# Attention plus gated MLP on one core: the second batch's q loaded ahead of the weights, w_sg in two loads, paired loads for the last batch, and a new written order of steps

## Chip, core and metric

The kernel runs on one core of one Trainium2 chip. The metric is the device time in microseconds of one execution. Engines are named as in the profile: PE is TensorE's matmuls and PEld its weight loads, DVE is VectorE, ACT is ScalarE, POOL is GpSimd and SP is SyncE, which here only issues DMAs. TensorE writes its results into PSUM, and other engines have to copy them out before the PSUM buffer can be used again.

## What is computed

There are two layers, one behind the other, on 4 batches of 768 positions. First comes attention with 8 heads of 64, where each position sees the last 128 positions and the first 4 ("sinks"):

```
scores = (q @ k^T) / 8;  keep = (pos_k < 4) | (0 <= pos_q - pos_k < 128)
a = softmax(where(keep, scores, -1e9));  x[b, s, 64*h:64*h+64] = a @ v
```

Then comes a gated MLP on x (768 x 512 for each batch):

```
h = gelu_tanh(x @ w_in)                     # 512 -> 1024, halves u and v of 512
v_n = (v - mean(v)) / sqrt(var(v) + 1e-6) * g_ln
v_s = w_sg @ v_n + b_sg                     # mixes the 768 positions
out = x + (u * v_s) @ w_out                 # 512 -> 512
```

All inputs are float32 in device memory. The matmuls run in bf16, and the loads that POOL issues convert on the way.

## The kernel before, in words

The whole program is one long list of short steps, the string STEPS (lines 16 to 64). Each step is a small function, called once with the numbers behind its name: batch first, then head pair, tile or half. The order of the list is the order of issue on every engine: each engine works through its own share of the list strictly in order, and what ties the engines together are semaphore waits that follow from who reads and writes which buffer. There is no scheduler at run time. A trailing letter A, D or P says which engine (ACT, DVE, POOL) does a copy, a mask or a product.

**Attention.** Heads go in pairs, four pairs p = 0..3 for each batch. LQ and LK load q and k (lines 191 to 213), LV loads v (line 216). For batches 0 to 2 (letter S in TURN, line 72), TQ and TK turn q and k with 12 TensorE transposes a pair (line 304), and EQ and EK copy the result out of PSUM (lines 221 and 223). For batch 3 (letter D) SP turns them with a DMA transpose (line 314), from buffers qn and kn; those are loaded one head at a time (line 198), two loads for each pair. KS picks the four sink columns of k (line 329), SK multiplies them with q (lines 338 and 344), SX takes the exponential (349). QK makes scores for two key tiles of one pair (358), EX takes the exponential (366), MK masks (DVE 373, POOL 377 and 381), AV multiplies with v for one half of the positions (398, 404, 408), and NR divides by the row sum and writes x (417, 418).

**MLP.** XT and XE turn x on TensorE and copy it out (427, 221/223); for batches 2 and 3 XD does it with a DMA transpose on SP (435). MV and MU are the two halves of x @ w_in (444, 496), with MA and UA as first parts of them, GV and GU their gelu (458, 512). BN, RS, NM and Z normalise v (467 to 487); RS is on POOL (475). WT and WE turn w_sg, six row tiles, once (519, 524). SP multiplies with w_sg (529), GT adds the bias (534), GM multiplies with u (539), OU multiplies with w_out (545), RA adds x (553), ST stores (556). HM(n) puts n extra matmuls of nothing ahead of a step (183).

**What sets the order.** PSUM is used through two rings of buffers: "sc" with 2 (QK, MV, MU) and "mm" with 4 (all other matmul results). The step that takes a buffer of a ring waits until the copy or product that read its last contents is done. The masked scores P have a ring of 8. The 1152 KB of w_sg arrive in one load (LWS, line 239) in a buffer that GM's products use later.

**POOL as a DMA queue.** Almost all loads are issued by POOL, in line with its masks, products and RS. There are eight DMA semaphores for them, handed out in turn, so a load waits until the load eight before it has landed, and everything behind it on POOL waits too:

```
   def LWS():
        return nc.gpsimd.dma_start(out=wsg_rows, in_=moe_w_sg.rearrange("(c p) f -> p c f", p=128))
```

The order of the loads before is: q and k of batch 0, v of batch 0, w_in (two halves, LW), w_sg, w_out (LWO), then q and k of batch 1 for pairs 0-1, v of batch 1, q and k of batch 1 for pairs 2-3, and so on. q and k of batches 1 and 2 come in loads of four heads (384 KB in bf16), v in loads of two heads (192 KB).

Of the kernel before, what the change touches and what calls it, by code (L numbers as in the profile page):

```python
# [9 lines left out]
BF16 = mybir.dt.bfloat16  # L10
# [18 lines left out]
GM.0.1.0.D LV.2.1 SP.0.0.1 GT.0.1.1 EK.1.1.A MK.1.0.0 QK.1.0.1 QK.1.0.2 GT.0.0.1 GM.0.1.1.P TQ.1.2 EX.1.0.1 TQ.1.3
EQ.1.2.D TK.1.3 GM.0.0.1.P EX.1.0.2 QK.1.1.1 TK.1.2 EK.1.3.D EQ.1.3.A MK.1.0.1.P QK.1.1.2 SP.0.1.3 EK.1.2.A MK.1.0.2.D  # L30
LQ.2.2 EX.1.1.1 SP.0.0.2 KS.1.0 LK.2.2 EX.1.1.2 GT.0.1.3 SK.1.0 LV.2.2 GT.0.0.2 QK.1.2.2 SX.1.0 QK.1.1.0 MK.1.1.2.D
SP.0.1.2 LV.2.3 EX.1.1.0 MK.1.1.1.D AV.1.0.1 EX.1.2.2 GM.0.1.3.P GT.0.1.2 AV.1.1.1 NR.1.0.1 GM.0.0.2.P QK.1.3.0 TK.2.0
NR.1.1.1 EX.1.3.0 TK.2.1 LQ.3.0 MK.1.2.2.D QK.1.3.2 TQ.2.1 EK.2.1.A EK.2.0.D QK.1.3.1 EQ.2.1.A SP.0.0.3 MK.1.3.0
LK.3.0 GM.0.1.2.D AV.1.0.0 GT.0.0.3 TQ.2.0 EX.1.3.1 NR.1.0.0 OU.0.5 MK.1.1.0 EX.1.3.2 LV.3.0 TQ.2.2 RA.0.5 EQ.2.0.A
TQ.2.3 QK.1.2.1 MK.1.3.2.D ST.0.5 QK.1.2.0 EQ.2.3.A AV.1.1.0 EQ.2.2.D MK.1.3.1.P OU.0.3 EX.1.2.0 NR.1.1.0 AV.1.3.0
EX.1.2.1 TK.2.3 RA.0.3 TK.2.2 LQ.3.1 NR.1.3.0 EK.2.3.A ST.0.3 QK.2.0.1 QK.2.0.0 MK.1.2.0 AV.1.3.1 EK.2.2.A XT.1.2
MK.1.2.1.P EX.2.0.1 NR.1.3.1 OU.0.4 XE.1.2.D EX.2.0.0 MK.2.0.1.P AV.1.2.0 RA.0.4 AV.1.2.1 NR.1.2.0 QK.2.0.2 ST.0.4
QK.2.1.1 EX.2.0.2 XT.1.0 LK.3.1 EQ.3.0 KS.2.0 XT.1.1 EX.2.1.1 SP.0.0.0 XE.1.0.D NR.1.2.1 MK.2.0.2.P QK.2.1.2 QK.2.1.0
XE.1.1.D SK.2.0 EX.2.1.2 MK.2.1.1.P GT.0.0.0 XT.1.3 EK.3.0 SX.2.0 MV.1.0 GM.0.0.0.D LV.3.1 XE.1.3.A MK.2.0.0 EX.2.1.0
MK.2.1.2.D LQ.3.2 AV.2.0.0 GM.0.0.3.D GV.1.0 MK.2.1.0 MV.1.2 EQ.3.1 LK.3.2 OU.0.2 LV.3.2 GV.1.2 BN.1.0 MV.1.1 LQ.3.3  # L40
EK.3.1 RA.0.2 OU.0.0 BN.1.2 GV.1.1 MU.1.2 ST.0.2 RA.0.0 RS.1.2 EQ.3.2 OU.0.1 GU.1.2 BN.1.1 LK.3.3 MU.1.1 LV.3.3 NM.1.2
MU.1.3 RA.0.1 GU.1.1 ST.0.0 EK.3.2 RS.1.1 Z.1.4.A NR.2.0.0 MU.1.0 Z.1.5.A NM.1.1 GU.1.3 Z.1.1.D AV.2.0.1 Z.1.2.D
GU.1.0 AV.2.1.1 Z.1.3.D ST.0.1 QK.2.2.0 Z.1.0.A NR.2.0.1 QK.2.2.1 AV.2.1.0 EX.2.2.0 NR.2.1.1 SP.1.1.0 NR.2.1.0
SP.1.0.3 GT.1.1.0 GM.1.1.0.D EQ.3.3 EX.2.2.1 SP.1.0.2 MK.2.2.0 GT.1.0.3 QK.2.3.1 MK.2.2.1.P QK.2.3.0 GT.1.0.2 EX.2.3.1
SP.1.0.1 EK.3.3 GM.1.0.3.D GM.1.0.2.D EX.2.3.0 AV.2.2.0 MK.2.3.1.P GT.1.0.1 SP.1.1.2 NR.2.2.0 QK.2.2.2 GM.1.0.1.D
QK.2.3.2 SP.1.0.0 MK.2.3.0 EX.2.2.2 GT.1.1.2 EX.2.3.2 AV.2.3.0 MK.2.2.2.D QK.3.1.0 GT.1.0.0 MK.2.3.2.P QK.3.0.2
AV.2.2.1 EX.3.1.0 NR.2.3.0 SP.1.1.1 GM.1.0.0.P EX.3.0.2 NR.2.2.1 XD.2.0 AV.2.3.1 GM.1.1.2.D MK.3.0.2.P GT.1.1.1 OU.1.2
NR.2.3.1 GM.1.1.1.P QK.3.1.1 RA.1.2 QK.3.1.2 OU.1.1 EX.3.1.1 MK.3.1.0 EX.3.1.2 SP.1.1.3 KS.3.0 ST.1.2 XD.2.1 RA.1.1
MK.3.1.2.P SK.3.0 QK.3.0.0 GT.1.1.3 SX.3.0 QK.3.0.1 OU.1.0 MK.3.1.1.D EX.3.0.0 GM.1.1.3.P AV.3.1.0 EX.3.0.1 RA.1.0
MV.2.0 MK.3.0.0 ST.1.0 MK.3.0.1.D ST.1.1 OU.1.3 GV.2.0 OU.1.5 RA.1.3 MV.2.2 ST.1.3 BN.2.0 MV.2.1 GV.2.2 RA.1.5 BN.2.2  # L50
ST.1.5 MU.2.2 GV.2.1 OU.1.4 BN.2.1 GU.2.2 RS.2.2 MU.2.0 NM.2.2 RS.2.1 RA.1.4 MU.2.3 GU.2.0 NR.3.1.0 ST.1.4 MU.2.1
Z.2.5.D GU.2.3 NM.2.1 Z.2.4.D Z.2.1.A Z.2.2.D AV.3.0.1 Z.2.0.D GU.2.1 QK.3.2.0 NR.3.0.1 AV.3.1.1 EX.3.2.0 Z.2.3.D
# [22 lines left out]
def kernel(  # L79
# [14 lines left out]
    nc = tc.nc  # L94
# [188 lines left out]
    def ZERO():  # L283
        for t in v_sb:
            nc.vector.memset(t[:, :, :, Dh:Dh + 1], 1.0)
        for t in ks_sink:
            nc.vector.memset(t, 0.0)
# [337 lines left out]
```

## Time and profile before

| | |
|---|---|
| median of 4 runs | 160.19 us (159.74 to 160.43) |
| the profiled execution | 159.3 us, of which the span of the profile is 157.6 us |
| TensorE clock granted, mean | 0.995 |
| busy in the span | PE 146.8, DVE 128.6, ACT 100.7, POOL 87.0 us |
| loads issued by POOL | 45600 packets, 77.3% of 16 engines' span |
| transfers issued by SP | 17648 packets, 28.0% |

Times in the profile count from the span's start. Busy time of PE is a union of pipelined matmuls, each of which is shown longer than the distance to the next one: six matmuls of SP are 0.97 us apart from start to start of the next group, though one is shown as 326 ns. Where the text below adds up matmul work, it uses these distances. A landing time of a load is the start of its issue plus the time from issue to landing.

### The profile page before, as it was taken

What the parts mean: (1) busy time and instruction counts of PE and PEld (TensorE: products, weight loads), DVE (VectorE), ACT (ScalarE), POOL (GpSimd) and SP (SyncE); (2) the same over time, 40 slices, a digit from 0 to 9 for tenths busy, and PEclk for the clock granted to TensorE, in tenths of its full rate; (3) what the DMA queues carried; (4) which work ended last, traced back from release to release, by engine and by line L of the source; (5) the groups of instructions that cost most, each with busy time, mean ns of one, the idle gap of its engine ahead of it and who ended that gap; (6) DMA issues with size and microseconds to landing.
All of it is one profiled execution on the core that took longest, in us unless ns stands there. A gap on an engine that the chain in (4) does not pass through costs nothing.

```text
span 157.6 us, 3835 instructions
## 1 busy us (share of the span) xinstructions
PE 146.8 (93%) x1522; PEld 86.7 (55%) x1522; DVE 128.6 (82%) x305; ACT 100.7 (64%) x118; POOL 87.0 (55%) x118
## 2 busy tenths in 40 slices
PE   4878989989999999999999999999999999999970
PEld 1444566655566667554575655455656644556530
DVE  4479899998699999959979997779899936976861
ACT  3689995369997798795599658655975124670000
POOL 7998890244899995998923485004046400409120
PEclk9999999999999999999999999999999999999998
DMA  5999999999999999999999159431001581030154
GB/s 160 171 186 165 195 209 209 206 233 178 180 198 173 196 153 213 187 173 140 210 218 174 17 100 152 169 116 66 5 0 24 115 265 69 0 120 14 55 184 166
DMA packets 63266, 22.70 MB, mean 144 GB/s; under 512 B 51472, under 2 KB 60176, under 8 KB 63248
## 3 DMA queue, kind: packets, MB, share of 16 engines
q0 software_dynamic: 45600, 11.80, 77.3%
q1 hardware_dynamic: 17648, 10.66, 28.0%
q8 instruction: 12, 0.20, 0.5%
q14 instruction: 6, 0.05, 0.1%
HBM read 24.81 MB, written 6.29 MB: 197 GB/s over the span
## 4 chain that ended last, share of the span: by engine, by line
PE 61%; DMA 24%; POOL 9%; issue 1%; DVE 1%; POOLq 1%; DVEq 0%
PE mm L529 16%; DMA k<-in_k_dram 13%; PE mm L545 12%; PE sc L496 11%; DMA v_sb<-in_v_dram 11%; PE sc L444 10%; PE sc L358 4%; PE mm L398 3%; POOL v_sb L216 2%; POOL k L194 2%; POOL q L194 2%; PE mm L404 2%; PE mm L408 1%; PE mm L304 1%; PE mm L427 1%
## 5 line engine op out<-in xcount | busy, mean ns | idle before, releaser
L366 ACT ACTIVATE P<-sc 128x1024 bf16<-128x1024 f32 (+1 forms) x48 | 43.6, 962 | 10.1 <-PE sc L358 9.3
L529 PE MATMUL mm<-wsgT,z 128*128 128x384 bf16 x192 | 34.2, 326 | 0.0
L529 PEld LDWEIGHTS <-z 128*128 128x128 bf16 x192 | 17.8, 98 | 12.2 <-issue 1.3
L545 PE MATMUL mm<-w_out_sb,wsg_gated 128*128 128x512 bf16 (+1 forms) x100 | 23.7, 371 | 0.9 <-POOL wsg_gated L539 0.9
L534 DVE SCALAR_TENSOR_TENSOR gtmp<-mm,g_sb,b_bc 128x384 bf16<-128x384 f32 x32 | 19.4, 613 | 4.6 <-PE mm L529 4.6
L496 PE MATMUL sc<-xT,w_in_sb 128*128 128x384 bf16 x128 | 22.8, 326 | 0.0
L444 PE MATMUL sc<-w_in_sb,xT 128*128 128x512 bf16 x96 | 22.5, 379 | 0.1
L553 DVE TENSOR_TENSOR ot<-mm,x_sb 128x512 f32<-128x512 f32 (+1 forms) x25 | 16.5, 666 | 7.3 <-PE mm L545 7.2
L373 DVE TENSOR_TENSOR P<-P,mask 128x1024 bf16<-128x1024 bf16 (+1 forms) x31 | 22.0, 725 | 0.4 <-ACT P L366 0.3
L377 POOL TENSOR_SCALAR_AFFINE_SELECT P<-P 128x512 bf16<-128x512 bf16 x17 | 11.1, 656 | 19.0 <-ACT P L366 12.7
L539 POOL TENSOR_TENSOR wsg_gated<-gtmp,uT 128x384 bf16<-128x384 bf16 x16 | 15.4, 966 | 11.1 <-DVE gtmp L534 11.0
L216 POOL DMA_DIRECT2D v_sb<-in_v_dram x16 | 16.5, 1040 | 7.1 <-DMA wsg_gated<-in_moe_w_sg_dram 5.5
L458 ACT ACTIVATE vt<-sc 128x1024 f32<-128x1024 f32 x12 | 12.2, 1023 | 12.5 <-PE sc L444 12.5
L512 ACT ACTIVATE uT<-sc 128x768 bf16<-128x768 f32 x16 | 12.7, 805 | 10.4 <-PE sc L496 10.4
L475 POOL TENSOR_TENSOR rs<-rs,neg_half 128x4 f32<-128x4 f32 (+1 forms) x8 | 7.1, 886 | 21.5 <-DVE rs L470 19.6
L418 DVE TENSOR_TENSOR x_sb<-mm,rcp 128x384 bf16<-128x384 f32 x32 | 17.8, 558 | 1.1
L467 DVE BATCH_NORM_STATS2 st<-vt 128x6 f32<-128x512 f32 x24 | 16.2, 674 | 2.9 <-ACT vt L458 2.9
L358 PE MATMUL sc<-qT,kT 64*128 64x256 bf16 x192 | 15.3, 263 | 2.2 <-ACT P L366 1.4
L496 PEld LDWEIGHTS <-w_in_sb 128*128 128x128 bf16 x128 | 12.3, 98 | 9.0
L398 PEld LDWEIGHTS <-P 128*128 128x128 bf16 x192 | 14.7, 98 | 4.5 <-issue 2.2
L398 PE MATMUL mm<-v_sb,P 128*128 128x65 bf16 x192 | 16.5, 194 | 0.3
L404 PE MATMUL mm<-v_sb,P 128*128 128x65 bf16 x160 | 15.5, 194 | 0.0
(73 smaller groups left out, 222.3 us busy)
## 6 DMA issues: line engine op xcount, KB each, us to landing
out_dram<-ot SPq DMA_DIRECT2D x23, 256.0 KB, 2.4
v_sb<-in_v_dram POOLq DMA_DIRECT2D x16, 192.0 KB, 9.5
q<-in_q_dram POOLq DMA_DIRECT2D x4, 384.0 KB, 15.9
k<-in_k_dram POOLq DMA_DIRECT2D x4, 384.0 KB, 14.7
wsg_gated<-in_moe_w_sg_dram POOLq DMA_DIRECT2D x1, 1152.0 KB, 15.9
w_in_sb<-in_moe_w_in_dram POOLq DMA_DIRECT2D x2, 512.0 KB, 9.9
qn<-in_q_dram POOLq DMA_DIRECT2D x8, 96.0 KB, 6.0
kn<-in_k_dram POOLq DMA_DIRECT2D x8, 96.0 KB, 5.5
```

The lines of the kernel that those rows point to most:

```text
L216: return nc.gpsimd.dma_start(out=v_sb[b % len(v_sb)][:, 2 * p:2 * p + 2, :, 0:Dh].rearrange("p h t d -> p (h t) d"), in_=v[b, 2 * p:2 * p ...
L358: nc.tensor.matmul(sc[:, hl, 256 * jl:256 * jl + n], kT[b, p][rows, 128 * j:128 * (j + 1)], qT[b, p][rows, 128 * j:128 * j + n], start=Tru ...
L366: nc.scalar.activation(out=pt[:, :, 0:w], in_=sc_ring[b, p, g][:, :, 0:w], func=AF.Exp, scale=scale)
L373: nc.vector.tensor_mul(pt[:, :, 0:w], pt[:, :, 0:w], m.unsqueeze(1).to_broadcast([128, 2, w]))
L398: nc.tensor.matmul(av[:, il, hl, :], P[b, p, i // 2][:, hl, 256 * (i % 2):256 * (i % 2) + 128], vb[:, h, i, :], start=first, stop=False)
L404: nc.tensor.matmul(av[:, il, hl, :], P[b, p, j // 2][:, hl, 256 * (j % 2) + 128:256 * (j % 2) + 256], vb[:, h, j, :], start=False, stop=False)
L418: nc.vector.tensor_mul(xs[:, 3 * half:3 * half + 3, 128 * p:128 * (p + 1)].rearrange("p t (h d) -> p t h d", h=2), av[:, :, :, 0:Dh], rcp. ...
L444: nc.tensor.matmul(hp[:, jl, :], xT[b][:, j, c, :], w_in_sb[:, c, d_half:2 * d_half], start=(c == 0), stop=(c == KD - 1))
L496: nc.tensor.matmul(hp[:, n, 0:NH], w_in_sb[:, c, 128 * dc:128 * (dc + 1)], xT[b][:, 3 * hf:3 * hf + 3, c, :], start=(c == 0), stop=(c == K ...
L529: nc.tensor.matmul(ps[:, 0:NH], z[b][:, si, 128 * dc:128 * (dc + 1)], wsgT[:, si, NH * hf:NH * (hf + 1)], start=(si == 0), stop=(si == NT ...
L534: nc.vector.scalar_tensor_tensor(out=gtmp.new((b, hf, dc)), in0=mm_ring["g", b, hf, dc][:, 0:NH], scalar=g_sb[:, dc:dc + 1], in1=b_bc[:, N ...
L545: nc.tensor.matmul(mm_ring["o", b, t][:, cols], gatedT[:, (2 * b + hf) % 3, dc, 128 * tl:128 * (tl + 1)], w_out_sb[:, dc, cols], start=(dc ...
```

## The change

The steps' functions stay as they are except for these:

- LWS takes a number: w_sg comes in two loads of three row tiles (576 KB each).
- For batch 3, q and k of two pairs now share one buffer (qn and kn have 2 buffers of twice the size), and a load brings two heads for it instead of one: 8 loads of 192 KB instead of 16 of 96 KB. A pair of batch 3 then holds heads 0 and 2, or 1 and 3 of the four, and AV and NR address its two heads with a stride (heads()).
- The sink product of batch 3 follows from that: KS writes into a new buffer ks_far, which ZERO clears with one more memset, and SK makes two accumulating matmuls of 64 columns for each half of the 128 rows, where it made four of 32 columns.
- LG, the load of b_sg, waits for the first half of w_sg, where it waited for the whole.
- The branch for letter R, which no batch used, is gone.

The list of steps is written anew. In its loads: POOL masks come ahead of the third load, q of batch 1, pairs 0-1, is loaded ahead of the last v load of batch 0 and of w_in; q and k for the other pairs of batch 1 follow right behind w_sg; w_out comes behind k of batch 1, v of batch 1 behind the first q of batch 2, and v of batch 2 ahead of its k. The first two casts of q and k (CQ, CK) go from ACT to DVE. Work given to engines, before and after, in steps:

| | before | after |
|---|---|---|
| copies of turned q and k (EQ, EK) on ACT / DVE | 15 / 9 | 17 / 7 |
| casts CQ, CK on ACT / DVE | 2 / 0 | 0 / 2 |
| masks (MK) on DVE / POOL | 31 / 17 | 28 / 20 |
| products (GM) on DVE / POOL | 16 / 16 | 15 / 17 |
| normalising (Z) on ACT / DVE | 10 / 14 | 9 / 15 |
| extra matmuls (HM) | 10 | 8 |

The core of the diff:

```diff
-HOLDS = "LG<LWS"
+HOLDS = "LG<LWS.0"
...
-    qn = Ring("qn", 4, [128, NT, 2, Dh], BF16)
-    kn = Ring("kn", 4, [128, NT, 2, Dh], BF16)
+    qn = Ring("qn", 2, [128, 2, NT, 2, Dh], BF16)
+    kn = Ring("kn", 2, [128, 2, NT, 2, Dh], BF16)
...
     def rows(ring, src, b, p):
-        t = ring.new((b, p))
-        return [nc.gpsimd.dma_start(out=t[:, :, hl, :], in_=src[b, 2 * p + hl].rearrange("(t p) d -> p t d", p=128))
+        t = ring.new((b, p // 2))
+        return [nc.gpsimd.dma_start(out=t[:, :, :, hl, :].rearrange("p k t d -> p (k t) d"),
+                                    in_=src[b, 2 * p + 2 * hl:2 * p + 2 * hl + 2].rearrange("h (t p) d -> p (h t) d", p=128))
                 for hl in range(2)][-1]
+
+    def heads(b, p):
+        return slice(2 * p - p % 2, 2 * p - p % 2 + 3, 2) if TURN[b][p] == "D" else slice(2 * p, 2 * p + 2)
...
-    def LWS():
-        return nc.gpsimd.dma_start(out=wsg_rows, in_=moe_w_sg.rearrange("(c p) f -> p c f", p=128))
+    def LWS(i):
+        return nc.gpsimd.dma_start(out=wsg_rows[:, NG * i:NG * (i + 1), :],
+                                   in_=moe_w_sg[128 * NG * i:128 * NG * (i + 1), :].rearrange("(c p) f -> p c f", p=128))
...
-        for t in ks_sink:
+        for t in (*ks_sink, ks_far):
             nc.vector.memset(t, 0.0)
...
         ps = fresh(mm_ring, ("s", b, p0))
         for p in range(HP):
+            if TURN[b][p] == "D":
+                r0 = 64 * (p // 2)
+                nc.tensor.matmul(ps[r0:r0 + 64, :], ks_far[:, 64 * p:64 * p + 64], qT[b, p][:, 256:768],
+                                 start=(p % 2 == 0), stop=(p % 2 == 1))
+                continue
```

The first part of the list, up to the first SP step, before:

```
 ZERO IDEN LQ.0.0 LK.0.0 LQ.0.1 FILL LK.0.1 LC MASK LQ.0.2 MASK0 CQ.0.0.A VSK LK.0.2 HM.7 TQ.0.0 CK.0.0.A LV.0.0
 ...
 QK.0.1.2 MK.0.0.1.D LW.1 SX.0.1 QK.0.1.1 MK.0.1.0 EX.0.1.2 AV.0.0.0 LWS TQ.0.3 EK.0.2.A NR.0.0.0 QK.0.0.2 EQ.0.3.A LWO
 ...
 LG LV.1.2 WT.3 GV.0.1 WT.5 WE.3 WT.4 WT.1 WE.5 MV.0.2 LV.1.3 WE.4 BN.0.1 MU.0.1 GV.0.2 WE.1 RS.0.1 WT.2 BN.0.2 GU.0.1
 TQ.1.0 TQ.1.1 EQ.1.0.A MU.0.2 LQ.2.0 EQ.1.1.A NM.0.1 WE.2 RS.0.2 Z.0.3.A TK.1.0 Z.0.0.D MU.0.3 GU.0.2 NM.0.2 EK.1.0.D
 Z.0.2.A Z.0.4.D WT.0 Z.0.1.A QK.1.0.0 Z.0.5.D TK.1.1 GU.0.3 WE.0 SP.0.1.0 LK.2.0 EX.1.0.0 LV.2.0 SP.0.1.1 GT.0.1.0
```

and after:

```
 ZERO IDEN LQ.0.0 LK.0.0 LQ.0.1 FILL LK.0.1 LC MASK VSK LK.0.2 MASK0 CQ.0.0.D LK.0.3 HM.7 TQ.0.0 CK.0.0.D LQ.0.2
 ...
 EX.0.3.1 QK.0.3.0 MK.0.1.0 LQ.1.2 EX.0.3.0 QK.0.2.1 MK.0.1.2.D LK.1.0 AV.0.1.0 MK.0.2.0 AV.0.1.1 EX.0.2.1 MK.0.3.1.P
 NR.0.1.0 QK.0.3.2 SX.0.3 QK.0.2.2 NR.0.1.1 EX.0.3.2 LK.1.2 TQ.1.0 MK.0.2.1.D XT.0.2 EX.0.2.2 LWO TQ.1.1 MK.0.3.0
 EQ.1.0.A AV.0.2.0 XE.0.2.D MK.0.3.2.P EQ.1.1.A NR.0.2.0 AV.0.3.0 XT.0.0 MK.0.2.2.P NR.0.3.0 AV.0.3.1 XE.0.0.D LQ.2.0
 XT.0.1 AV.0.2.1 NR.0.3.1 MA.0.0 XE.0.1.D NR.0.2.1 MV.0.0 VSM.1 LV.1.0 XT.0.3 GV.0.0 VSM.3 UA.0.0 VSM.2 MU.0.0 LG WT.1
 LV.1.1 XE.0.3.A BN.0.0 WT.2 WT.0 GU.0.0 MV.0.2 WE.2 WE.1 MV.0.1 WE.0 LV.1.2 GV.0.2 BN.0.2 MU.0.3 GV.0.1 WT.3 BN.0.1
 RS.0.2 GU.0.3 WT.5 TQ.1.3 LV.1.3 TQ.1.2 EQ.1.3.A MU.0.1 WE.5 RS.0.1 EQ.1.2.A WE.3 NM.0.2 MU.0.2 GU.0.1 LQ.2.2 Z.0.4.D
 NM.0.1 Z.0.5.A Z.0.1.D TK.1.0 Z.0.3.D GU.0.2 TK.1.1 LV.2.0 Z.0.2.D TK.1.2 EK.1.0.A Z.0.0.D TK.1.3 EK.1.1.D EK.1.2.A
 QK.1.0.2 QK.1.0.0 SP.0.0.2 EK.1.3.A EX.1.0.0 LV.2.1 KS.1.0 WT.4 SP.0.0.0 GT.0.0.2 WE.4 SK.1.0 GT.0.0.0 SP.0.1.2
```

The last stretch, batch 3's MLP, has the same steps in nearly the same order.

## The prediction

> **What bounds the kernel now.** I read busy time by stretch first, since the page's shares average over stages with different limits.
>
> ```profile
> core 0: us, PE busy (x) PEld busy (x) DVE busy (x) ACT busy (x) POOL busy (x), PEclk, DMA share, GB/s
> 0.00:8.00 8.00, 5.32 (x48) 2.54 (x50) 3.56 (x17) 3.84 (x5) 7.11 (x17) 1.00 0.83 166
> 8.00:24.00 16.00, 13.43 (x227) 8.81 (x224) 14.29 (x31) 15.09 (x19) 14.73 (x20) 1.00 1.64 189
> 24.00:39.60 15.60, 14.97 (x164) 9.32 (x161) 14.45 (x38) 9.85 (x13) 4.74 (x5) 1.00 1.46 206
> 39.60:59.80 20.20, 20.02 (x311) 12.79 (x309) 18.14 (x36) 17.89 (x23) 19.16 (x23) 1.00 1.90 179
> 59.80:111.00 51.20, 51.20 (x470) 29.52 (x471) 44.64 (x113) 36.78 (x43) 27.88 (x38) 1.00 1.17 147
> 111.00:149.30 38.30, 38.30 (x304) 22.06 (x302) 30.10 (x68) 17.26 (x20) 12.46 (x16) 1.00 0.23 64
> ```
>
> From 59.8 to 149.3 PE is never idle at full clock: only less matmul work or closer matmuls could shorten it, and the change leaves that work alone. What can be won lies before 60. In 8 to 24 (attention of batch 0) ACT is busy 15.09 of 16.0, DVE 14.29, POOL 14.73.
>
> The waits come next. Weight loads show PE's waits better than matmuls:
>
> ```profile
> 34.26 0.70 PEld L304 LDWEIGHTS <-q 128*64 128x64 bf16 x24 [0.59 <-DMA q<-in_q_dram]
> 36.62 0.36 PEld L304 LDWEIGHTS <-k 128*64 128x64 bf16 x12 [0.47 <-DMA k<-in_k_dram]
> ...
> 40.85 0.62 DVE L534 SCALAR_TENSOR_TENSOR gtmp<-mm,g_sb,b_bc 128x384 bf16<-128x384 f32 x1 [1.29 <-PE mm L529]
> ```
>
> So q and k of batch 1 arrive late, 1.1 us in all. The chain of waits puts far more on loads (k 13%, v 11%), but those are transfers lying under PE work; I don't count them. Then the loads and POOL's own waits:
>
> ```profile
> wsg_gated<-in_moe_w_sg_dram POOLq DMA_DIRECT2D x1, 1152.0 KB, 15.9
> w_out_sb<-in_moe_w_out_dram POOLq DMA_DIRECT2D x1, 512.0 KB, 17.6
> ...
> 29.25 1.03 POOL L216 DMA_DIRECT2D v_sb<-in_v_dram  x1 [5.49 <-DMA wsg_gated<-in_moe_w_sg_dram]
> ```
>
> Issue plus landing time gives the queue: w_in 20.2 and 22.7, w_sg 28.6, w_out 31.1, q and k of batch 1 34.2 and 36.6, the last v of batch 2 58.5. Loads land back to back, so each costs its distance to the one before: v 1.5, w_in 2.3, w_sg 5.9, w_out 2.5, a four-head q or k 1.7 to 2.75 (I take 2.2).
>
> **The measure.** I sum matmul work in list order from start-to-start distances in PE's timeline (TQ, TK 0.43; QK 0.27; AV 0.36 and 0.54; XT, WT, SK 0.33; MV 1.73; MU 1.30; SP 0.97; OU 0.86) and call "lag" the time minus this work. Before: XT.0.3 done at 27.1 with 19.1 of work, lag 8.0; TK.1.1 at 39.6 with 30.5, lag 9.1; TK.2.2 at 59.8 with 49.5, lag 10.3; OU.3.1 at 148.25 with 136.4, lag 11.9; last matmul 153.8 with 140.8, lag 13.0. After has 140.1: two extra matmuls less (0.33 each, where PE waits anyway).
>
> **The change, part by part.**
>
> *Start.* CQ and CK move from ACT (0.83 each) to DVE. DVE's nearest row is Z, 541 ns for 512 float32 elements, so at most 0.81 for 768, at least 0.44 by the mask copy below (0.29 for 512 of bf16). MASK0 ends at 4.66, so CQ ends at 5.1 to 5.5. TQ.0.0 starts at 5.36 now, behind HM's matmuls; cost 0 to 0.15, and nothing once TQ.0.1 waits for its load at 7.3. I take 0. Clearing ks_far is one more memset, nearest row 0.33, under DVE's wait for the mask.
>
> [...] The trace:
>
> ```profile
> 3.89 0.72 POOL L194 DMA_DIRECT2D q<-in_q_dram  x1
> ...
> 3.99 0.29 DVE L274 COPY mask<-mask 128x512 bf16<-128x512 bf16 x1 [0.68 <-POOL mask L270]
> ...
> 5.05 0.71 POOL L194 DMA_DIRECT2D k<-in_k_dram  x1
> ```
>
> The issue beside a DVE copy took 0.72, the one without 0.71: no delay for a bf16 copy; a float32 cast isn't shown. [...] I take 0.
>
> *Attention of batch 0.* ACT loses EQ.0.1, EQ.0.3 and XE.0.2 there (0.74 each by distance, 2.2 us), and takes EQ.1.0, EQ.1.1 behind its last EX. DVE gains two copies (0.87) and an XE (0.47) and loses a mask (0.6): 15.9 of 16, so it takes over as the limit. By hand from KS.0.0 at 7.8 (EQ.0.1 8.8, VSM 9.8, EK.0.1 10.7, three masks and EK.0.3 to 13.4, EQ.0.2 14.3, EQ.0.3 15.1, then NR, MK and XE as AV delivers) the last NR ends at 25.1, now 25.76. ACT's last EX ends at 20.6 instead of 22.2. On POOL, MK.0.3.2 and MK.0.2.2 stand behind two loads that wait: LK.1.2 for q of batch 1 (18.8), LWO for the last v (20.3). They end at 22.1 and 23.1; AV.0.2.1 needs the latter, then MV.0.0 starts at 24.5. PE ends MU.0.0 at 27.0 with 19.3 of work, the transposes of q of batch 1 among them: lag 7.7.
>
> *w_sg in halves.* WT.1 waits for the first half: 28.6 - 2.95 + 2.2 (q now ahead) = 27.85. PE waits 0.8: lag 8.5. Without q ahead it would not wait here; the trade is for the waits at 34 and 36.6. Second half 30.8, used at 33.6. LG also waits for the first half only; b_sg isn't needed before 41.
>
> *q, k, w_out.* Landings, by the same distances forward: q 33.0, k 35.2 and 37.4, w_out 39.7, q of batch 2 41.5, v of batch 1 43 to 47.5; and back from the last v at 58.5, as now since the packets are the same: k of batch 2 55.1 and 57.0. PE wants TK.1.0 at 37.6 and TK.1.2 at 38.5 (margin 1.1), TQ.2.0 at 44, AV.1.0.0 at 48, OU.0.0 at 54, TK.2.0 at 57.2, TK.2.3 at 58.5. None is late. TK.1.3 ends at 39.4 with 30.9 of work: lag 8.5, against 9.1.
>
> *39.4 to 60.* KS.1.0 now stands early in DVE's order and waits for the ACT copy of EK.1.3 (40.7): 1.3 us idle with all of DVE's GT, masks and NR queued behind it, and PE waits for those through its four mm buffers. From 41.0 to TK.2.2 DVE has 17.9 us (8 GT of 0.65, 8 masks of about 0.57, 6 NR of 0.72, 5 GM, 2 RA, 2 XE, WE, KS), which ends at 58.9 without a gap, just where PE is. It was 90% busy in this stretch; at 90% it takes 19.9, to 60.9. PE stall 0 to 1.5; I take 0.5, since three EK and EQ copies (0.87 each) have left DVE here. TK.2.2 ends at 59.9 with 50.0: lag 9.9, a lead of 0.4 over 10.3.
>
> *Loads of batch 3.* 16 issues of 0.86 become 8 of 1.03 (the v row): POOL loses 5.3 us (13.5 - 8.2) and gets back three masks of 1.2 and one GM of 0.93, all with room. On SP the DMA transposes come later: four of them between the stores of batch 0's last tiles, EK.3.0 last at about 83, landing by 88.5; QK.3.0 wants it near 92. Cost 0.
>
> *SK.3.0.* Four matmuls of 32 columns become four of 64.
>
> ```profile
> L344 PE MATMUL mm<-qT,ks_sink x12: 389/390/390, 47.4 to 95.8; 128*32 128x512 bf16 x12
> ```
>
> In the chain, four take 0.33 together: four abreast. [...] The transposes of 64 columns gain about 1.5x (36 ns instead of 55). I take +0.2, once, in the saturated stretch; bounds 0 and 0.5.
>
> *60 to the end.* Lag grew by 1.6 up to 148 and 1.1 in the tail, where OU.3.5 waits for the last GM on POOL (0.87); the tail is the same. DVE has 4.7 us less work left here, so no new limit. I keep both.
>
> Sum: 9.9 + 2.7 + 140.1 + 0.2 = 152.9 for the last matmul, 0.9 before 153.8. The profiled execution of 159.3 (span 157.6, 1.7 around it) becomes 158.4; it lay 0.9 under the median. On the median: 160.2 - 1.0 = 159.2.
>
> **Rivals.**
> - *More gain (158.2).* If DVE keeps pace to 60 (the 0.5 falls away) and its lighter load closes a third of the 1.6 of late lag growth: 1.0 + 0.5 + 0.5 = 2.0. For: DVE idles 6.6 us in 59.8:111. Against: PE shows no idle to close there.
> - *No change (160.2).* DVE is the bound to 60: at its 90% the stretch costs 1.5 instead of 0.5, which eats the gain. For: it was never above 93% in any stretch.
> - *Slower (161.4).* The load queue runs late, and WT.1 at 27.85 has no cover, so PE is late one for one, with TK.1.2 (margin 1.1) behind. [...] It decides from 1.0 late. Against: eight loads in flight hold over 15 us of work.
>
> **How the numbers follow.** Forecast 0.38, more gain 0.14, no change 0.20, slower 0.28. Within 0.5% (about 0.8 us, what a measurement can tell from no change) means 159.4 to 161.0. Of the forecast 0.34 lies below that and 0.04 in it; of no change 0.16 in it and 0.02 on either side. So faster 0.34 + 0.14 + 0.02 = 0.50, same 0.20, slower 0.28 + 0.02 = 0.30. The forecast's own range is 158.4 to 160.2; for 8 in 10 it runs from 157.6 (all stalls at their low ends) to 161.7 (the slower case with SK at 0.5).
>
> **What would show it.** Right: no wait of PE for q and k near 34 to 39, TK.1.3 done near 39.4; the wait moved to WT.1 near 27.8; DVE above 93% in 39 to 60, with one idle of about 1.3 before KS. Wrong: first w_sg half after 29, PE waiting on DVE copies in 8 to 24, waits at QK.3 for a DMA transpose, or a gap in PE after 60.

## The result and the profile after

The changed kernel takes 159.52 us in the median of 44 runs (158.97 to 164.26), the kernel before 160.21 us in 63 runs. The ratio is 0.9967, with a 95% interval of 0.9955 to 0.998: about 0.5 us won, where 1.0 was forecast. In this and all later ratios only fast runs are compared (the slow ones of the changed kernel, 161.8 and above, show a granted clock of 0.979 to 0.989, the others 0.989 to 1.0), so that a ratio is not the quotient of the two medians. When the changed kernel was run once more (experiment 11), its ratio was 0.9992 [0.9967, 1.0018], so that the gain is near the edge of what can be measured.

The profiled execution of after took 159.89 us (span 158.2), that of before 159.3 (span 157.6). The first lies 0.37 above its median and the second 0.9 below: the trace of after is 0.6 us longer than that of before, though its median is 0.7 shorter. The traces show where time goes, but the difference of their spans is not the difference of the kernels.

Busy time by stretch, after (columns as in the prediction):

```profile
8.00:24.00 16.00, 12.78 (x228) 8.31 (x224) 14.76 (x31) 14.52 (x18) 14.22 (x19) 1.00 1.59 173
24.00:39.60 15.60, 15.33 (x157) 9.60 (x159) 13.61 (x38) 8.81 (x12) 9.04 (x13) 1.00 1.26 217
39.60:59.80 20.20, 19.89 (x303) 12.79 (x298) 18.20 (x43) 18.85 (x24) 15.31 (x19) 1.00 2.10 173
59.80:111.00 51.20, 51.20 (x479) 29.21 (x476) 44.09 (x105) 36.98 (x44) 25.50 (x35) 1.00 1.25 150
111.00:149.30 38.30, 38.30 (x303) 21.92 (x302) 29.47 (x67) 18.20 (x21) 13.85 (x19) 1.00 0.25 69
```

From 59.8 to 149.3 PE is never idle, as before. In 24 to 39.6 it is busier (15.33 against 14.97): the waits for q and k are gone. In 8 to 24 it is less busy (12.78 against 13.43): that stretch got worse, though the forecast had it better. (The two lists don't have quite the same steps in a stretch, so this is a hint, not a measure.)

PE's waits, from the timeline of its weight loads (start, duration, what was loaded, and in brackets the idle time ahead of it and who ended it):

```profile
12.29 0.36 PEld L308 LDWEIGHTS <-q 128*64 128x64 bf16 x12 [0.43 <-DMA q<-in_q_dram]
13.30 0.36 PEld L308 LDWEIGHTS <-q 128*64 128x64 bf16 x12 [0.65 <-DMA q<-in_q_dram]
...
24.06 0.10 PEld L407 LDWEIGHTS <-P 128*128 128x128 bf16 x1 [0.58 <-POOL P L386]
29.28 1.01 PEld L528 LDWEIGHTS <-wsg_gated 128*128 128x128 bf16 x18 [0.59 <-DMA wsg_gated<-in_moe_w_sg_dram]
...
95.85 0.14 PEld L349 LDWEIGHTS <-ks_far 128*64 128x64 bf16 x3 [0.42 <-DVE ks_far L335]
96.44 0.11 PEld L349 LDWEIGHTS <-ks_far 128*64 128x64 bf16 x1 [0.45 <-DVE ks_far L335]
...
151.75 2.06 PEld L554 LDWEIGHTS <-wsg_gated 128*128 128x128 bf16 x14 [0.97 <-POOL wsg_gated L548]
```

Nothing stands between 29.28 and 95.85 for q or k: those waits have indeed gone, and one at WT.1 (29.28) has come for them. New are the waits for the early q (12.29, 13.30) and, not foreseen at all, one for KS on DVE at 96.44. (The 0.42 at 95.85 is put down to KS too, but a gap of 0.42 stands there in experiment 12 as well, where KS is done 1.1 us ahead, and one of 0.32 in the kernel before: only the 0.45 is a wait for KS.) The cause is seen when DVE's and POOL's timelines are laid beside each other. DVE, after:

```profile
20.50 1.94 DVE L382 TENSOR_TENSOR P<-P,mask 128x1024 bf16<-128x1024 bf16 x2
...
94.35 2.04 DVE L335 TENSOR_TENSOR ks_far<-kT,halfsel 128x8 bf16<-128x8 bf16 x4
```

POOL, after:

```profile
20.19 0.65 POOL L386 TENSOR_SCALAR_AFFINE_SELECT P<-P 128x512 bf16<-128x512 bf16 x1
20.79 1.10 POOL L390 TENSOR_SCALAR_AFFINE_SELECT P<-P 128x512 bf16<-128x512 bf16 x1
...
94.18 0.63 POOL L386 TENSOR_SCALAR_AFFINE_SELECT P<-P 128x512 bf16<-128x512 bf16 x1
94.77 0.42 POOL L390 TENSOR_SCALAR_AFFINE_SELECT P<-P 128x256 bf16<-128x256 bf16 x1
95.15 0.63 POOL L386 TENSOR_SCALAR_AFFINE_SELECT P<-P 128x512 bf16<-128x512 bf16 x1
95.74 0.63 POOL L390 TENSOR_SCALAR_AFFINE_SELECT P<-P 128x512 bf16<-128x512 bf16 x1
```

And the same four products of KS.3.0 in the kernel before, while POOL had nothing to do:

```profile
94.69 0.39 DVE L329 TENSOR_TENSOR ks_sink<-kT,halfsel 128x8 bf16<-128x8 bf16 x4
```

Four products of 8 elements take 0.39 us alone and 2.04 us beside POOL's selects. One by one, they end at 94.83, 95.20, 95.80 and 96.39, each within 0.02 us of the end of a select (94.81, 95.19, 95.78, 96.37). Two masks take 1.28 us alone and 1.94 beside a select, and the second of the two selects takes 1.10 instead of 0.65. So DVE and POOL seem to hold each other up. This became the main theory of the experiments.

### The profile page after: what moved, and what is told of

It is laid out like the page before. It is cut to its first block, busy times and chain, and to the rows that moved or that the text cites. A ratio compares the mean times of both kernels' runs of the same rounds, so it can differ in the third digit from the quotient of the medians.

```text
span 158.2 us, 3811 instructions
## 1 busy us (share of the span) xinstructions
PE 146.7 (93%) x1520; PEld 86.5 (55%) x1520; DVE 127.7 (81%) x303; ACT 100.2 (63%) x117; POOL 86.4 (55%) x118
## 4 chain that ended last, share of the span: by engine, by line
PE 72%; DMA 10%; POOL 7%; ACT 4%; DVE 2%; issue 2%; POOLq 1%; DVEq 0%
PE mm L538 18%; PE mm L554 12%; PE sc L453 12%; PE sc L505 12%; DMA wsg_gated<-in_moe_w_sg_dram 10%; PE sc L367 6%; PE mm L407 3%; PE mm L308 3%; POOL v_sb L221 3%; PE mm L413 2%; PE mm L417 2%; ACT kT L226 1%; POOL k L195 1%; PE mm L528 1%; ACT P L375 1%
## 5 line engine op out<-in xcount | busy, mean ns | idle before, releaser
L538 PE MATMUL mm<-wsgT,z 128*128 128x384 bf16 x192 | 35.1, 326 | 0.0
L538 PEld LDWEIGHTS <-z 128*128 128x128 bf16 x192 | 17.5, 98 | 12.2 <-issue 1.9
L548 POOL TENSOR_TENSOR wsg_gated<-gtmp,uT 128x384 bf16<-128x384 bf16 x17 | 15.9, 939 | 13.0 <-DVE gtmp L543 6.7
L484 POOL TENSOR_TENSOR rs<-rs,neg_half 128x2 f32<-128x2 f32 (+1 forms) x8 | 6.9, 864 | 28.1 <-DVE rs L479 25.6
L453 PE MATMUL sc<-w_in_sb,xT 128*128 128x512 bf16 x96 | 22.0, 379 | 0.0
L467 ACT ACTIVATE vt<-sc 128x1024 f32<-128x1024 f32 x12 | 12.2, 1025 | 14.4 <-PE sc L453 12.7
L386 POOL TENSOR_SCALAR_AFFINE_SELECT P<-P 128x512 bf16<-128x512 bf16 x20 | 13.1, 657 | 11.6 <-ACT P L375 11.6
L562 DVE TENSOR_TENSOR ot<-mm,x_sb 128x512 f32<-128x512 f32 (+1 forms) x25 | 16.3, 664 | 3.7 <-PE mm L554 3.6
L382 DVE TENSOR_TENSOR P<-P,mask 128x1024 bf16<-128x1024 bf16 (+1 forms) x28 | 18.4, 686 | 0.2
L407 PE MATMUL mm<-v_sb,P 128*128 128x65 bf16 x192 | 16.8, 194 | 1.5 <-DMA v_sb<-in_v_dram 0.8
L413 PE MATMUL mm<-v_sb,P 128*128 128x65 bf16 x160 | 15.7, 194 | 0.0
## 6 DMA issues: line engine op xcount, KB each, us to landing
k<-in_k_dram POOLq DMA_DIRECT2D x4, 384.0 KB, 14.2
```

The costliest lines, as they stand in the source:

```text
L382: nc.vector.tensor_mul(pt[:, :, 0:w], pt[:, :, 0:w], m.unsqueeze(1).to_broadcast([128, 2, w]))
L407: nc.tensor.matmul(av[:, il, hl, :], P[b, p, i // 2][:, hl, 256 * (i % 2):256 * (i % 2) + 128], vb[:, h, i, :], start=first, stop=False)
L413: nc.tensor.matmul(av[:, il, hl, :], P[b, p, j // 2][:, hl, 256 * (j % 2) + 128:256 * (j % 2) + 256], vb[:, h, j, :], start=False, stop=False)
L453: nc.tensor.matmul(hp[:, jl, :], xT[b][:, j, c, :], w_in_sb[:, c, d_half:2 * d_half], start=(c == 0), stop=(c == KD - 1))
L538: nc.tensor.matmul(ps[:, 0:NH], z[b][:, si, 128 * dc:128 * (dc + 1)], wsgT[:, si, NH * hf:NH * (hf + 1)], start=(si == 0), stop=(si == NT ...
```

## The experiments

**Theory.** The gain comes from the order of the loads (w_out behind k, so that PE doesn't wait for q and k at 34 to 37). Half of what was forecast is lost again, because DVE's masks and small products and POOL's selects don't run side by side. **Rivals:** the casts on DVE hold up the load queue; or the new functions (paired loads, 64-column sink products) cost time by themselves.

**1. Casts back on ACT.** Whether the casts on DVE lengthen POOL's load issues, tried by itself:

```diff
- CQ.0.0.D ... CK.0.0.D
+ CQ.0.0.A ... CK.0.0.A
```

> The kernel after, with the two first casts of q and k back on ScalarE; nothing else is changed. Theory A (the casts on VectorE hold up GpSimd's load issues, which took 1.04 us each beside them instead of 0.72): the issues of the third and fourth load fall back to 0.7 each, w_sg's first half lands 0.6 to 1.5 earlier than 29.3, and the time is 0.3 to 1.0 under that of the kernel after (0.990 to 0.995 of the kernel before). Theory B (the casts cost nothing, the load queue's lateness has another source): the issues stay at 1.04 or the landing doesn't move, time within 0.3 of the kernel after (0.995 to 0.999).

Measured: ratio to the kernel before 0.9969 [0.9941, 0.9996], against 0.9967 with the casts on DVE: no gain. POOL's issues of two k loads, with the casts on ACT:

```profile
4.41 1.43 POOL L195 DMA_DIRECT2D k<-in_k_dram  x2
```

and with the casts on DVE:

```profile
4.41 2.08 POOL L195 DMA_DIRECT2D k<-in_k_dram  x2
```

So the casts do lengthen the issues, by 0.65 us in this trace and in that of experiment 12, and by 0.2 to 0.4 in the other later ones; all queue entries behind them move. In the traced execution the first half of w_sg landed at 28.4 instead of 29.2. It brought nothing, and in this trace one sees why:

```profile
17.26 3.15 DVE L382 TENSOR_TENSOR P<-P,mask 128x1024 bf16<-128x1024 bf16 x3
...
21.72 2.51 DVE L382 TENSOR_TENSOR P<-P,mask 128x1024 bf16<-128x1024 bf16 x2
```

Five masks took 5.7 us, against 3.0 to 3.9 in most traces of nearly the same list (5.4 in that of experiment 7): with the loads earlier, POOL's selects came to lie beside them. WT.1 started only at 30.2, behind a late MU.0.0, though its rows lay there from 28.4.

**2 and 3. Functions without the list, and the list without the functions.** The changed functions with the old list (LWS.0 and LWS.1 one behind the other where LWS stood):

> The functions of the kernel after (paired loads and the 64-column sink product for batch 3), with the list of steps of the kernel before; w_sg's two loads stand next to each other. Theory A (the list makes the gain, the functions cost a little in the sink product, 0.2 to 0.6): 1.001 to 1.004 of the kernel before. Theory B (the gain comes from the eight load issues saved on GpSimd, or from the half of w_sg): 0.996 to 0.998.

Measured: 163.07 us, ratio 1.0162 [1.0122, 1.0202]. Much more than expected. And the new list with the functions of before for batch 3 (four loads of one head for each two pairs, four sink products of 32 columns):

```diff
-        t = ring.new((b, p // 2))
+        ts = [ring.new((b, p)), ring.new((b, p + 1))]
...
-                for hl in range(2)][-1]
+                for k in range(2) for hl in range(2)][-1]
```

> The list of the kernel after, with the functions of the kernel before for batch 3 (one head for each load, four sink products of 32 columns); w_sg in two loads as the list has it. Theory A (the list makes the gain): 0.993 to 0.997 of the kernel before, the sink product of batch 3 back at 0.4 us. Theory B (the paired loads make the gain): 0.999 to 1.004, with GpSimd's masks and products after 57 late by up to 5 us of issues.

Measured: ratio 1.0153 [1.0088, 1.0217]. Neither half of the change is worth anything alone. What fails in this one is seen in the weight loads (the traced execution is longer than the runs compared, so it shows the place, not the size):

```profile
70.36 0.10 PEld L546 LDWEIGHTS <-wsg_gated 128*128 128x128 bf16 x1 [3.32 <-POOL wsg_gated L540]
```

OU.0.2 waits 3.3 us for GM.0.1.3 on POOL, which stands behind twice as many load issues of batch 3. In the changed kernel there is no such wait. The paired loads, which I had costed at nothing on PE's path, are what lets the new list put these loads there.

**4. q of batch 1 back behind w_sg** (LQ.1.0 moved behind LWS.1):

> The kernel after, with the load of q of batch 1 (pairs 0-1) moved behind w_sg's second half; its transposes stay where they are in the list. Theory A (the early q trades a wait at w_sg for one at q): TensorE waits for q from 20 to about 30, with the rest of batch 0 behind it in line, 1.03 to 1.06 of the kernel before. Theory B (q's place matters little, since eight loads are in flight anyway): 0.995 to 1.005.

Measured: 172.93 us, ratio 1.0778 [1.0734, 1.0823].

```profile
33.16 0.61 PEld L308 LDWEIGHTS <-q 128*64 128x64 bf16 x12 [12.97 <-DMA q<-in_q_dram]
```

The list puts TQ.1.0 among the steps of batch 0, so PE stands for 13 us until q lands. The place of this load is no gain by itself. It is a condition for where TQ.1.0 stands.

**5. KS.3.0 later**, behind POOL's selects:

```diff
- EX.3.0.0 KS.3.0 OU.1.0 ... SK.3.0 RA.1.0 QK.3.0.2 SX.3.0 QK.3.1.0 OU.1.2
+ EX.3.0.0 OU.1.0 ... RA.1.0 KS.3.0 QK.3.0.2 QK.3.1.0 SK.3.0 SX.3.0 OU.1.2
```

> The changed kernel with KS.3.0 moved behind RA.1.0, and SK.3.0 and SX.3.0 behind QK.3.1.0. In the changed kernel the four products of KS.3.0 took 2.04 us, 0.45 to 0.67 each, while POOL ran four affine selects back to back; in the kernel before, and with the old list, they took 0.39 together while POOL was idle. Theory A (DVE's small products stand still while POOL's selects run, and PE pays for it at SK.3.0): KS takes at most 0.8 us, no wait before SK.3.0, the four sink products take 0.56 us instead of 0.93 to 0.99, and the time falls by 0.3 to 0.7 us, ratio to the kernel before 0.991 to 0.995. Theory B (what is won at SK.3.0 is lost at a later wait, or KS is slow for its own sake): ratio 0.995 to 1.000.

Measured: ratio 0.9986 [0.9963, 1.0009]: no gain, theory B for the time. KS.3.0 took 0.39 us, as the mutual hold-up demands, but now stood behind two sums that wait for PE, and SK.3.0 waited 0.65 us for it all the same. From QK.2.0 to the last matmul it took 93.5 us in the trace, in the changed kernel 93.2.

**6. w_out ahead of the second q of batch 1** (LWO moved ahead of LQ.1.2):

> The changed kernel with w_out loaded ahead of the second half of q of batch 1 (LWO ahead of LQ.1.2), everything else left. Theory A (the place of w_out behind k is what took the waits for q and k away): q and k of batch 1 land 2.5 us later, at about 37.5, 39.5 and 41.5; PE waits about 1.5 to 2.5 us for k before 42; time 1.0 to 2.5 us above the changed kernel, ratio to the kernel before 1.003 to 1.012. Theory B (the queue's order doesn't decide, since PE is behind DVE and ACT there): ratio 0.995 to 1.001, waits below 0.5 us.

Measured: ratio 1.0084 [1.0054, 1.0114], theory A.

```profile
38.37 0.70 PEld L307 LDWEIGHTS <-q 128*64 128x64 bf16 x24 [1.94 <-DMA q<-in_q_dram]
```

The wait for q is back, with 1.94 us. Against the changed kernel it is 1.2% or 1.9 us, the size of the wait. The move also put a load more ahead of POOL's selects; PE waited 1.33 us for a mask on DVE at 23.96. But that is not what counts: the transposes of q start as soon as q has landed (38.3), 2.6 us later than in the first trace of the changed kernel, and the first scores behind them are 2.6 later as well. So, within the new list, the place of w_out is worth about 1.9 us. The old list wasn't tried with w_out moved alone.

**7. w_sg in one load** in the changed kernel:

> The changed kernel with w_sg in one load again, at the place of the first half. Theory A (the first half alone lets WT.1 start): WT.1 waits until about 32.0 instead of 29.3, PE stands still for about 3 us instead of 0.6, part of it made good later since the waits at 34 to 41 were already gone; time 1.5 to 2.7 us above the changed kernel, ratio to the kernel before 1.006 to 1.014. Theory B (one load less in the queue of eight lets POOL go on earlier, which makes up for the wait): ratio 0.995 to 1.002.

Measured: 163.03 us, ratio 1.0168 [1.012, 1.0216]. The size is that of theory A, but in the trace two things come together. WT.1's matmuls started at 32.27 and w_sg had landed at 31.9: PE didn't wait for it. It was late already:

```profile
21.39 3.17 DVE L380 TENSOR_TENSOR P<-P,mask 128x1024 bf16<-128x1024 bf16 x2
```

One load fewer, and POOL was 1.3 us earlier with its selects (22.02 to 24.00, four on end), so that two masks on DVE took 3.17 us instead of 1.94, and AV behind them waited 1.85 us. Without that PE would have stood waiting for w_sg instead, and could have started WT.1 only 0.4 us earlier. Either cause alone puts it at about 32, where the halves let it start at 28.8 to 29.3. That w_sg in one load lands about 3 us late is thus shown; what the halves would be worth with everything behind them rearranged is open.

**8. The kernel before with only w_sg in two loads:**

```diff
- LWS
+ LWS.0 LWS.1
```

> The kernel before with nothing changed but w_sg in two loads, one right behind the other. With the changed functions and the old list the time was 1.6% above the kernel before; its POOL issued each load only when the load eight places earlier had landed, so that one load more moved the next issues to 14.6, 16.6 and 18.1 instead of 13.5, 14.2 and 15.6, and PE waited 1.2 and 1.0 us for two masks on POOL behind them. Theory A (the extra load in the queue is the whole cost): the same two waits of about 1 us, ratio 1.011 to 1.019. Theory B (the paired loads of batch 3 or the sink products of 64 columns cost it): no such waits, ratio 0.997 to 1.004.

Measured: 162.01 us, ratio 1.0111 [1.0069, 1.0152], theory A: about 1.8 us of the 2.6 of experiment 2 come from one more load in the queue. Not quite by the waits expected, though. POOL issued q of batch 1 at 16.0 instead of 14.2 (each load waits for the one eight places earlier, this one 1.03 us for a v), so its selects moved from 17.9 to 20.6, next to two masks of DVE. POOL, then DVE:

```profile
20.62 0.65 POOL L377 TENSOR_SCALAR_AFFINE_SELECT P<-P 128x512 bf16<-128x512 bf16 x1
21.22 0.64 POOL L381 TENSOR_SCALAR_AFFINE_SELECT P<-P 128x512 bf16<-128x512 bf16 x1
21.81 0.64 POOL L377 TENSOR_SCALAR_AFFINE_SELECT P<-P 128x512 bf16<-128x512 bf16 x1
22.40 1.09 POOL L381 TENSOR_SCALAR_AFFINE_SELECT P<-P 128x512 bf16<-128x512 bf16 x1
```

```profile
20.51 3.52 DVE L373 TENSOR_TENSOR P<-P,mask 128x1024 bf16<-128x1024 bf16 x2
```

Two masks took 3.52 us, in the kernel before 1.79 and alone 1.28. The first of them took 2.49 us, to 23.0, while three selects went by, though its record starts 0.11 us ahead of theirs; the second took 1.11 beside the fourth, which took 1.09 itself. PE's waits for masks behind that were 1.03, 0.65 and 0.51 us. What the other 0.8 us of experiment 2 come from wasn't tried.

**9 to 11.** Three kernels beside each other. First the wait in the tail, which both kernels have:

```diff
- GM.3.1.2.P
+ GM.3.1.2.D
```

> The changed kernel with the last product of gtmp and uT (GM.3.1.2) on DVE instead of POOL. In its trace OU.3.5 waits 0.97 us for this product: 0.91 us on POOL from 150.79 on, where DVE's products of this shape take 0.35 and DVE has just made its input. Theory A (that wait sets the end): the wait falls to about 0.4 us, time 0.4 to 0.7 us below the changed kernel, ratio to the kernel before 0.992 to 0.995. Theory B (the output's stores or DVE's sums behind it set the end): ratio 0.996 to 0.998, as the changed kernel.

Measured: 0.9972 [0.9943, 1.0002], the changed kernel in the same comparison 0.9992. The time can't tell it from theory B. The trace can: OU.3.5 started 1.41 us behind the matmuls ahead of it instead of 1.94.

```profile
150.82 2.56 PE L553 MATMUL mm<-w_out_sb,wsg_gated 128*128 128x256 bf16 x14 [0.16 <-DVE wsg_gated L547]
```

Then the four masks that POOL makes in batch 0, on DVE:

> The changed kernel with the four masks of batch 0 that POOL makes (MK.0.1.1, MK.0.3.1, MK.0.3.2, MK.0.2.2) on DVE instead. In the traces so far a DVE mask of 128x1024 takes 0.65 to 0.69 us alone, and up to 1.1 (changed kernel), 2.1 and 2.6 us where POOL's selects run at the same time, and the selects lengthen too, from 0.65 to 1.1. Theory A (DVE's masks and POOL's selects can't run side by side, so a mask on POOL wins little): with no select on POOL between 8 and 28 no DVE mask there takes over 0.75 us, and although DVE has 2.5 us more to do it loses only 1 to 1.8 us; ratio to the kernel before 1.000 to 1.008. Theory B (the masks are slow for another reason, such as their inputs coming late): some masks still take over 1 us, and the time rises by the whole 2.5 us or more, ratio above 1.010.

Measured: ratio 1.0009 [0.9983, 1.0036], theory A.

```profile
17.64 2.35 DVE L381 TENSOR_TENSOR P<-P,mask 128x1024 bf16<-128x1024 bf16 x4
21.30 1.28 DVE L381 TENSOR_TENSOR P<-P,mask 128x1024 bf16<-128x1024 bf16 x2
```

With no select on POOL every mask there takes 0.55 to 0.7 us. DVE got 2.5 us more work, and the kernel lost 0.3 to 0.7 us (against the ratios 0.9992 and 0.9967 of the changed kernel). Two things make the loss small, and they are not told apart: a mask handed to POOL can take back from DVE a part of what it gives (0.66 us on the two masks at 20.50 in the first trace of the changed kernel), and PE had to wait for w_sg anyway. MU.0.0 ended about 0.7 and 1.4 us later than in the two traces of the changed kernel, WT.1 started only 0.2 and 0.7 later.

And the changed kernel once more:

> The changed kernel once more, nothing altered, for a second trace of it: the first was 0.37 us above its median, that of the kernel before 0.9 below, so that the two traces stand in the wrong order. Theory A (single executions differ in the load queue and in how DVE's masks and POOL's selects fall together): ratio 0.995 to 0.998 again, but first loads, waits and masks between 6 and 28 differ by 0.5 to 1.5 us from the first trace, while from 60 on the two agree within 0.3 us. Theory B (the differences lie elsewhere): the first 28 us agree, and the difference arises later.

Measured: ratio 0.9992 [0.9967, 1.0018], just above what theory A gave. Its traced execution of 160.01 us bears out where single executions differ: no mask of batch 0 was held up this time (the two at 20.57 took 1.28 us), two k loads landed 1.5 us later than in the first trace, w_sg 0.5 earlier, and WT.1 started half a microsecond earlier.

```profile
28.78 1.01 PEld L528 LDWEIGHTS <-wsg_gated 128*128 128x128 bf16 x18 [0.72 <-DMA wsg_gated<-in_moe_w_sg_dram]
```

KS.3.0 was slow again (0.45 to 0.67 us a product): this one is no accident of an execution. From 61 on the two traces agree within about 0.1 us (OU.3.5 at 151.86 and 151.76).

Where PE's first scores of batch 1 (QK.1.0) and those of batch 2 start, in the timelines of the kernels with nearly this list, tells more than any one of them:

| | QK.1.0 | QK.2.0 | between |
|---|---|---|---|
| after, first and second trace | 41.08, 40.58 | 61.09, 61.20 | 20.01, 20.62 |
| casts on ACT (1) | 42.12 | 62.14 | 20.02 |
| KS later (5), tail (9), both (12) | 40.58, 40.66, 41.23 | 60.65, 60.68, 61.24 | 20.07, 20.02, 20.01 |
| masks on DVE (10) | 41.41 | 61.42 | 20.01 |
| w_out first (6), w_sg in one (7) | 43.63, 44.05 | 63.65, 64.61 | 20.02, 20.56 |

Seven of nine stretches take the same 20.0 us, whenever they start (experiments 3 and 4, not in the table, take 20.0 and 20.6). With PE busy for 19.89 of 20.20 us there and DVE for 18.20, it is most likely PE's own work that sets the time from 41 on; in two of the longer stretches PE does wait for DVE (0.91 us for a Z in experiment 7, 0.35 for an NR in the second trace). What an execution or an edit loses before 41 is not made good behind it.

The same holds one step further ahead. From WT.1 to QK.1.0 it is 11.8 to 11.95 us in eight of the nine traces (13.8 in experiment 6, with the wait for q between). And WT.1 starts at whichever comes later: the landing of w_sg's first half (both traces of after, experiments 5 and 12) or the end of MU.0.0 on PE (1, 6, 7, 9 and 10).

**12. Both remedies**: the tail of experiment 9, and the mask MK.3.1.2, which POOL makes beside KS.3.0, on DVE behind it:

```diff
- GM.3.1.2.P
+ GM.3.1.2.D
- QK.3.0.0 MK.3.1.2.P EX.3.0.1 ... RA.1.0 QK.3.0.2
+ QK.3.0.0 EX.3.0.1 ... RA.1.0 MK.3.1.2.D QK.3.0.2
```

> Two edits of the changed kernel together: GM.3.1.2 on DVE, which took 0.5 us from the wait in the tail, and the mask MK.3.1.2, which POOL makes while DVE runs KS.3.0, moved to DVE behind RA.1.0. Theory A (KS.3.0 is slow only beside POOL's selects, and SK.3.0 waits only for KS.3.0): the four products of KS.3.0 take about 0.4 us instead of 2.0, the waits of 0.42 and 0.45 us at SK.3.0 go, the four sink products take 0.56 us instead of 0.93; with the tail 0.7 to 1.1 us below the changed kernel, ratio to the kernel before 0.989 to 0.994. Theory B (what is won at SK.3.0 comes back at the next wait, as where KS was only moved): only the tail's gain, ratio 0.993 to 0.998.

Measured: 159.08 us against 160.38 of the kernel before in the same comparison, ratio 0.991 [0.9871, 0.9949]. That is theory A's range and better than both kernels, though the interval reaches into theory B's (0.993 to 0.998); the trace below decides. DVE:

```profile
94.49 0.39 DVE L334 TENSOR_TENSOR ks_far<-kT,halfsel 128x8 bf16<-128x8 bf16 x4
```

PE, here:

```profile
96.00 0.63 PE L348 MATMUL mm<-qT,ks_far 128*64 128x512 bf16 x4
```

and PE in the changed kernel:

```profile
95.85 0.99 PE L349 MATMUL mm<-qT,ks_far 128*64 128x512 bf16 x4
```

KS.3.0 is back to 0.39 us although DVE has a mask more to make, and SK.3.0 waits for KS no longer: of the two waits that were to go, the 0.45 is gone, while a gap of 0.42 stays ahead of the first sink product, now put down to a sum on DVE. The next matmuls start 0.56 us behind the start of the sink products instead of 0.93. From QK.2.0 to the last matmul it is 93.2 us in both traces of the changed kernel (and in those of experiments 1, 6, 7 and 10), 92.7 with the tail alone and 92.2 here: 0.5 for the tail and 0.5 for KS and its mask, of which 0.37 stand at SK.3.0.

## Why the prediction came out as it did

The direction was right, and the gain was half of what was forecast (0.5 instead of 1.0 us on the ratio). By its steps, with the trace of after:

- **q, k and w_out: right.** No wait of PE for q or k between 30 and 60; experiment 6 brings it back with 1.94 us when w_out goes ahead. The landings were 1.6 to 2.1 us later than forecast (q 35.1, k 37.0 and 39.0), which used the margin up, but PE was later too.
- **w_sg in halves: the wait was right, its time wrong, and this is the term that the time at 41 shows.** PE waits 0.59 us at WT.1 (0.72 in the second trace), forecast 0.8; but the half lands at 29.2 and 28.7, not at 27.85. WT.1 starts with the landing, and TK.1.3 ends as much too late as the load (by 1.4 and 0.9 us), as the rival "slower" had it; "first w_sg half after 29", a sign of being wrong, came in the first trace. Had the half landed in time, PE would still have been about 1.1 and 0.4 us late by its own work (next point): the two don't add. The queue is late early on: its first eight loads, the same in both lists though in another order, have landed by 17.5 and 16.5, in the kernel before by 15.1. Why is not shown; the casts are a part at most (16.3 without them).
- **Attention of batch 0: failed.** MU.0.0 was to end at 27.0 with lag 7.7; it ends at 28.9, and at 28.3 in the second trace. The step summed DVE's work by hand with undisturbed durations ("the last NR ends at 25.1"; measured 26.8 and 26.4). Two things are missing in it. The new order puts v of batch 0 behind all q and k, so that PE waits for the two last q (0.43 and 0.65) and for the first v (0.8). And DVE's masks beside POOL's selects are longer: 0.66 us in the first trace, nothing in the second, 2.6 in that of experiment 1. In the two traces of after this lateness lies under the wait for w_sg, so the hold-up of batch 0's masks doesn't explain the half that was lost there; in experiments 1, 7 and 10 it is MU.0.0 that sets WT.1. In no trace did QK.1.0 start before 40.6, where the forecast had TK.1.3, just ahead of it, done at 39.4.
- **The casts: wrong, without effect.** I took 0, though no row showed a float32 cast. The issues became 0.2 to 0.65 us longer: in the first trace of after the issue beside the two casts took 1.36 us, the next three 0.72 each, and it ended at 5.77, 0.15 us behind the second cast (5.62). The 161.4 of the rival "slower", and with it the 161.7 at the end of the range, counts 1.2 us for the casts, which no run shows: 0.65 was the most that two issues grew by, and the end of the kernel didn't move by it (experiment 1).
- **39.4 to 60: right in size, wrong in cause.** Lag was to grow by 1.4 from TK.1.3 to TK.2.2; it grew by 1.2 (40.8 with 30.9 of work to 61.1 with 50.0). But DVE was not above 93% busy: it was 90% (18.20 of 20.2), KS.1.0 idled 0.32 us, not 1.3, since Z and an EK copy, later than forecast, filled the time ahead of it, and the constant 20.0 us of the table above speak for PE itself filling this stretch. The 1.2 are then small gaps between its matmuls rather than one stall behind DVE.
- **Loads of batch 3: the cost of 0 on PE's path was right**; that the list depends on their number was missed (experiment 3).
- **SK.3.0: mis-sized.** +0.2 (0 to 0.5) was forecast for the wider products; with KS in time they take 0.56 instead of 0.33, so that this term was right to 0.03. But KS costs SK.3.0 another 0.37 us, which the step did not look at: 0.6 in all, and experiment 12 gets the 0.37 back.
- **60 to the end: right.** Lag grew by 3.1 from TK.2.2 to the last matmul, forecast 2.9 with SK.

The sum put the last matmul's end at 152.9; in the trace it is 154.3 (151.76 + 2.56). Of these 1.4, all stand at TK.1.3 already, from w_sg's landing; the next stretch took back 0.2 and the rest lost 0.2 to SK. That the median came out only 0.3 us above the forecast, though the trace is 1.4 above, is a matter of the two traced executions: the 0.9 which the prediction put between the trace of before and its median is not a constant of this kernel (for after it is -0.4). So that the number came so near is in part luck: a path 1.4 us too long, and 1.3 us of the difference between trace and median against it. (Two slips are small beside that: the last step takes 1.0 off where the sum gives 0.9, and the last v of batch 2 lands at 58.9, not at 58.5, in the trace of before.) How much of before's good first 40 us was luck isn't known: there is one trace of it. I also can't show how the net 0.5 us divides: the parts that were taken out alone, the casts aside, make the changed kernel 1.2 to 8.1% slower, far more than the gain, because list, loads and functions fit only together.

## What to carry to other kernels

Before work is moved from DVE to POOL, lay the two timelines beside each other: in this kernel bf16 tensor-tensor operations on DVE and selects on POOL took longer beside each other (two masks 1.94 to 3.52 us instead of 1.28, four products of KS 2.04 instead of 0.39, a select 1.10 instead of 0.65), so the move pays most where DVE would not be working on such operations at that moment, and a tiny DVE operation that TensorE waits for has to be kept clear of POOL's selects. Where POOL also issues the loads, one more load moves POOL's later work (in experiment 8 its selects from 17.9 to 20.6), so that splitting a load has to be tried together with what stands behind it in the queue. Where a step waits for two things, here a load and the engine's own work, find the later one before working on either: lateness of the other is hidden (in experiment 1 the half of w_sg landed 0.8 us earlier, and WT.1 started 0.9 later). And one trace of each kernel does not give a difference of half a percent (here the trace of after is 0.6 us longer, its median 0.7 shorter): use it for places, and the repeated times for sizes.

## What the hardware did that I had not expected

- A 128x1024 bf16 mask on DVE takes 0.68 to 0.71 us alone; with POOL's selects beside it single ones took up to 1.1 us (after), 1.2 (before), 2.1 (experiment 1), 2.5 (8) and 2.6 (7). The four products of KS.3.0 in the first trace of after look as if each had one select to wait for, since they end 0.01 to 0.02 us behind a select; but a mask that waits for one select of 0.65 would take about 1.3, and in experiment 8 one took 2.49 us, as if three selects had gone first. One mask was slow with no select beside it: 1.40 us in before (at 48.53, beside the issue of a v load and a GM on POOL), where most masks beside load issues take the usual 0.68. What holds these up is open.
- In the trace of experiment 4 PE stands still from 20.2 to 33.2. After it has begun again its weight loads are slow for another 3.4 us: the 12 at 33.16 take 0.61 us, where 12 of the same kind take 0.36 in the changed kernel, and single ones of P take 0.13 to 0.14 up to 36.5 and 0.10 from 36.6 on. The mean granted clock of that execution was 0.955, against 0.995 in the trace of after. A long wait of PE can so cost more than its own length; how much of the 12.7 us is due to it was not tried.
- Load landings move between executions of one program: the second and third k load of batch 0 landed at 8.7 and 9.6 in the first trace of after, and at 10.1 and 11.1 in the second, though their issue began no later there (4.40 and 5.30, against 4.41 and 5.77).
